# A Nystrom attention with a folded feed-forward network on one core: every stage cut into one step per engine, and a new written order

## The chip, the cores and the metric

The kernel runs on one core of a Trainium2 chip. A core has five engines that work side by side, each with its own queue of instructions that it takes strictly in order: TensorE (PE in the profile; its weight loads are shown as PEld), VectorE (DVE), ScalarE (ACT), GpSimd (POOL) and SyncE (SP), which here only issues transfers. Engines wait for each other through semaphores. The metric is the device time of one execution in microseconds; lower is better. The time given is the median of several executions.

## The reference

Eight batches of eight heads, 576 positions of 64 numbers each, go through a Nystrom approximation of attention with 32 landmarks; its output goes through a feed-forward network whose two halves are multiplied.

```python
q_lm = q.reshape(B, H, m, S // m, D).mean(axis=3)      # m = 32
k_lm = k.reshape(B, H, m, S // m, D).mean(axis=3)
A = sm(q, k_lm)          # sm: softmax of scaled products
Bm = sm(q_lm, k_lm)
C = sm(q_lm, k)
Z = Bm^T / (norm1(Bm) * norminf(Bm) + 1e-6)
for _ in range(6):
    Z = 2 * Z - Z @ Bm @ Z
attn = A @ Z @ C @ v
x = attn, heads side by side                            # 4608 x 512
h = (x @ w1) * (x @ w2) @ w3                            # 512 -> 1024
out = h @ w_out                                         # 1024 -> 512
```

## The kernel before

*Folding.* As nothing stands between w3 and w_out, the kernel first multiplies them into one matrix w34 (`fold`). w_out is split into a high and a low float16 half (`split`: ACT makes the high half at L510, DVE the low half at L511). Each 128 rows of w3 are turned by PE in two halves of four transposes (`turn` inside `fold`, L517) and split likewise (ACT L522, DVE L523). `product` multiplies them, three matmuls for each of 8 x 8 blocks (high by high, high by low, low by high, L530), into one PSUM bank per eight blocks, which ACT copies out (L533). Twelve matmuls on a tile of zeros (L599) stand at the start.

*Attention, per batch.* q and k come in through POOL's queue (L107), v through SP's (L126, L131). DVE turns q and k (`turn`, L143). `landmarks` sums groups of positions (DVE for batch 0, POOL for the others, L206 to L216). `exchange` swaps halves between partitions (by PE and ACT for batches 0 and 1, by small transfers on SP for the others). `scores_b` makes the 32 x 32 scores, `scores_c` and `scores_a` the long ones (32 matmuls of 32 x 32 each, L274 and L322), with exponentials on ACT (L255, L282, L328) and a DVE transpose (L284). `norms` (PE L290, DVE L293 to L297) and `squares` (PE L305) start the inverse; `inverse` has six steps (PE L399, then DVE L405 and, after DVE, ACT L410, which give the next step its operands). The inverse runs for one batch or two at once: CHAINS are (0), (1, 2), (3, 4), (5, 6), (7). `values` multiplies by v in three parts of 24 float32 matmuls (L344) and takes the sums in eight more (L349); the profile shows each float32 matmul as two, each with a weight load of its own, so that one batch's values are 320 rows on PE. `denominators`, `inverted`, `mixed` and `normalise` (PE L362, DVE L369, ACT L374, DVE L376, PE L382, DVE L385) give the scaled left factor `ahat`. `landmark_values` (PE L421, ACT L426, DVE L427) gives the middle factor `zt`.

*Network, per batch.* `project` multiplies `zt` by w1 or w2 (PE L442; ACT L446 or DVE L448 copy out): G0 and G2 are of w1, G1 and G3 of w2. `up` multiplies that by `ahat` (PE L455, four matmuls for each of 16 words): the w1 side is copied by ACT (L459), the w2 side multiplied into it by DVE (L461). `down` multiplies 128 positions by w34 (PE L495, eight matmuls), ACT copies out (L499), SP stores (L502). The last of the 36 `down` blocks is done in two halves.

*PSUM.* There are three tiles "big" of two banks, one "small" and one "acc", handed out in turn in the order of the text. A stage that takes a tile waits until the stage that had it has been read.

*The order.* Nothing schedules at run time or at build time: `manual_schedule` keeps the order in which the Python code emits. The string ORDER at the head has 575 words; the loop at L656 calls one function for each, for example `U3a.2` (`up`, eighth 3, w1 side, batch 2), `I4.1` (fifth step of the inverse of the chain of batch 1), `W0.17` (half a `down` block) or `F` (the next block of the fold). A function emits all of its work at once, its PE matmuls and behind them the ACT, DVE or POOL operations on their result. So one word fixes the place of that work on every engine's queue, relative to all other words. What stands before the loop (loads of w3, w_out, q, k of batches 0 and 1, w1 and w2, and DVE's constants at L162) is emitted first, in the order of the code; POOL's loads of q and k wait there behind a copy (`gate`, L603) that needs a tile of w_out.

Of the kernel before, what the change touches and what calls it, by code (L numbers as in the profile page):

```python
# [32 lines left out]
F F F F F F F F F F F F F TK0.0 F F F F F TQ0.0 TQ1.0 F F L3.3 F TK1.0 F F F F F SK0.0 SK1.0 F F  # L33
SQ0.0 P.4 F F F F L3.5 F L3.7 F F TQ0.1 TK0.1 SQ1.0 F F L3.6 TK1.1 F E.0 F B.0 F C0.0 SK0.1 N.0
F F F A0.0 R.0 FV.0 TQ1.1 F SK1.1 F I0.0 F F D.0 I1.0 F I2.0 Y0.0 Y1.0 SQ0.1 Y2.0 LK0.2 F X.0 F
I3.0 LK1.2 F F F I4.0 V0.0 V1.0 SQ1.1 LQ0.2 LQ1.2 E.1 F LK0.3 TK0.2 TK1.2 F LK1.3 I5.0 F V2.0
LV0.2 F TQ0.2 TQ1.2 A0.1 Z.0 SK0.2 LV0.1 LV1.1 F M0.0 LV2.1 F LV3.1 D.1 Y0.1 Y1.1 Y2.1 G0.0 G1.0
G2.0 M1.0 SK1.2 F SQ0.2 TK0.3 G3.0 TK1.3 C0.1 X.1 F F F F U0a.0 U0b.0 U1a.0 U1b.0 U2a.0 U2b.0
LQ0.3 TQ0.3 LQ1.3 LK0.4 U3a.0 LV1.2 V0.1 U3b.0 SQ1.2 E.2 U4a.0 U4b.0 B.1 U5a.0 U5b.0 N.1 V1.1
SK0.3 V2.1 R.1 U6a.0 U6b.0 TQ1.3 U7a.0 I0.1 M0.1 LK1.4 LQ0.4 U7b.0 W0.0 SK1.3 I1.1 W1.0 I2.1  # L40
A0.2 LV2.2 TK0.4 LV3.2 W0.1 I3.1 TK1.4 W1.1 I4.1 M1.1 LQ1.4 W0.2 TQ0.4 I5.1 W1.2 SQ0.3 SQ1.3
TQ1.4 Z.1 SK0.4 E.3 SK1.4 SQ0.4 LV0.3 C0.2 G0.1 D.2 G1.1 G2.1 W0.3 Y0.2 G3.1 V0.2 V1.2 Y1.2 V2.2
LV0.4 Y2.2 U0a.1 U0b.1 LV1.3 LK0.5 U1a.1 U1b.1 LV1.4 LK1.5 X.2 U2a.1 U2b.1 U3a.1 U3b.1 Z.2 SQ1.4
E.4 U4a.1 U4b.1 U5a.1 G0.2 TK0.5 U5b.1 U6a.1 U6b.1 M0.2 LQ0.5 LQ1.5 W1.3 U7a.1 LV2.3 U7b.1 LV3.3
M1.2 W0.4 G1.2 G2.2 G3.2 B.3 TK1.5 W1.4 U0a.2 A0.3 W0.5 U0b.2 U1a.2 LV2.4 D.3 Y0.3 Y1.3 SK0.5
U1b.2 Y2.3 C0.3 W1.5 LK0.6 U2a.2 U2b.2 U3a.2 W0.6 X.3 U3b.2 U4a.2 N.3 SK1.5 V0.3 V1.3 V2.3 R.3
U4b.2 TK0.6 W1.6 LV3.4 U5a.2 U5b.2 W0.7 TQ0.5 U6a.2 I0.3 M0.3 LK1.6 TQ1.5 W1.7 I1.3 SQ0.5 LQ0.6
U6b.2 W0.8 I2.3 W1.8 I3.3 U7a.2 U7b.2 W0.9 I4.3 M1.3 W1.9 I5.3 A0.4 LQ1.6 Z.3 C0.4 W0.10 G0.3
G1.3 G2.3 D.4 W1.10 Y0.4 LV0.5 SQ1.5 G3.3 E.5 LV1.5 U0a.3 U0b.3 Y1.4 W0.11 TK1.6 Y2.4 U1a.3
# [18 lines left out]
def kernel(  # L68
# [93 lines left out]
    def constants():  # L162
# [6 lines left out]
        for h in range(4):  # L169
            sl = slice(32 * h, 32 * h + 32)  # L170
            nc.vector.memset(mask4[sl, h, :], 1.0)
            for qd in range(2):
                nc.vector.tensor_copy(out=eye[sl, qd, :], in_=ident[sl, sl])
                nc.vector.memset(onesq[sl, qd, :, qd, h:h + 1], 1.0 / X64)
# [531 lines left out]
```

## Time and profile before

| | us |
|---|---|
| median of three executions | 264.64 (264.03 to 265.34) |
| profiled execution, first to last instruction (span) | 261.8 |
| median less span | 2.9 |
| PE busy | 251.5 |
| DVE busy | 173.8 |
| ACT busy | 134.7 |
| POOL busy | 103.2 |

The costliest groups on PE are `up` (L455, 512 matmuls, 73.1 us busy), `down` (L495, 264 matmuls into acc, 67.2) and the fold's products (L530, 168 into acc, 41.3). Busy times of groups overlap, since matmuls are pipelined.

By stretches of the span:

| stretch, us | PE busy | DVE busy | ACT busy | share of the 16 DMA engines |
|---|---|---|---|---|
| 0 to 10 | 8.29 | 8.70 | 5.07 | 0.81 |
| 10 to 50 | 39.48 | 26.16 | 16.84 | 1.06 |
| 50 to 100 | 46.48 | 36.24 | 23.81 | 0.73 |
| 100 to 180 | 79.74 | 60.74 | 48.30 | 0.72 |
| 180 to 262 | 77.51 | 41.98 | 40.72 | 0.38 |

A row of the profile gives line, engine, operation, output and inputs, shapes and count; behind the bar the busy time, the mean time of one in ns, and the idle time of the engine just before such instructions, with what ended it. A row of the timeline gives the start, the time taken, and in brackets the idle time before. "issue" means that the profile shows nothing that the engine waited for.

### The profile page before, as it was taken

The page shows a single profiled execution, that of the slowest core. Times are in us where ns is not written, and L with a number is a line of the kernel's source. Part 1 is how long each engine was busy: PE and PEld are TensorE (multiplying, and loading weights), DVE is VectorE, ACT ScalarE, POOL GpSimd, SP SyncE. Part 2 cuts the span into 40 slices and gives each one's busy share as a digit, 9 for nine tenths or more (in the row PEclk, how much of TensorE's full clock was granted, in tenths as well). Part 3 has the DMA queues.
Part 4 walks back from the last instruction along what each step waited for, and adds up shares of the span by engine and source line. Part 5 has one row for each costly group of instructions (what it writes and reads, how often), then busy time and mean ns, then how long its engine had stood idle before and what let it go on. Part 6 is the DMA issues. An engine that isn't in the chain of part 4 may idle for free.

```text
span 261.8 us, 10518 instructions
## 1 busy us (share of the span) xinstructions
PE 251.5 (96%) x4578; PEld 148.7 (57%) x4578; DVE 173.8 (66%) x352; ACT 134.7 (51%) x305; POOL 103.2 (39%) x134
## 2 busy tenths in 40 slices
PE   7999999998989999999999999999999999999993
PEld 3455554454556558557654674766476556656642
DVE  8765887556958687788856958767775656464410
ACT  4543236343652565576449546746646555455531
POOL 3630018998981999027092597504400000000000
PEclk9999999999999999999999999999999999999999
DMA  6999998999963448976668496933640713222355
GB/s 236 333 243 284 245 248 191 183 137 240 175 105 50 120 101 167 216 195 114 131 100 162 101 214 150 161 58 86 147 86 3 173 43 80 45 62 61 81 118 127
DMA packets 25070, 37.78 MB, mean 144 GB/s; under 512 B 4672, under 2 KB 13120, under 8 KB 25024
## 3 DMA queue, kind: packets, MB, share of 16 engines
q1 hardware_dynamic: 14704, 24.65, 36.9%
q0 software_dynamic: 9728, 11.54, 28.1%
q10 hardware_dynamic: 592, 0.92, 1.1%
q8 instruction: 36, 0.59, 1.0%
q14 instruction: 10, 0.08, 0.1%
HBM read 38.80 MB, written 9.44 MB: 184 GB/s over the span
## 4 chain that ended last, share of the span: by engine, by line
PE 89%; DVE 4%; ACT 3%; issue 1%; DMA 1%; SPq 0%; DVEq 0%; ACTq 0%
PE big L455 23%; PE acc L495 22%; PE acc L530 14%; PE big L442 5%; PE big L344 5%; PE big L399 4%; PE big L517 2%; PE small L530 2%; PE big L382 2%; PE small L421 2%; PE big L274 1%; PE big L495 1%; PE big L322 1%; DVE ab L461 1%; PE small L248 1%
## 5 line engine op out<-in xcount | busy, mean ns | idle before, releaser
L455 PE MATMUL big<-ahat,gt 128*128 128x288 f16 x512 | 73.1, 287 | 0.7 <-DVE ab L461 0.6
L495 PE MATMUL acc<-w,ab 128*128 128x512 f16 x264 | 67.2, 380 | 0.0
L461 DVE TENSOR_TENSOR ab<-a_sb,big 128x576 f16<-128x576 f16 x64 | 48.0, 750 | 27.2 <-ACT a_sb L459 16.8
L455 PEld LDWEIGHTS <-gt 128*128 128x128 f16 x512 | 48.3, 98 | 21.1 <-issue 3.1
L459 ACT CAST a_sb<-big 128x576 f16<-128x576 f32 x64 | 40.8, 640 | 33.9 <-PE big L455 32.9
L206 POOL TENSOR_TENSOR tr<-qkT 128x1024 f32<-128x1024 f16 x14 | 29.7, 2123 | 70.0 <-DVE qkT L143 69.8
L530 PE MATMUL acc<-wsp,w3t 128*128 128x512 f16 x168 | 41.3, 380 | 0.7 <-ACT w L533 0.5
L495 PEld LDWEIGHTS <-ab 128*128 128x128 f16 x280 | 25.3, 98 | 24.9 <-issue 3.5
L499 ACT ACTIVATE o_sb<-acc 128x512 f32<-128x512 f32 x33 | 19.8, 599 | 19.5 <-PE acc L495 19.1
L530 PEld LDWEIGHTS <-w3t 128*128 128x128 f16 x192 | 18.1, 98 | 18.9 <-issue 1.3
L143 DVE STREAM_TRANSPOSE qkT<-qkn 128x576 uint32<-128x576 uint32 x32 | 24.0, 763 | 2.0 <-DMA qkn<-in_k_dram 2.0
L448 DVE TENSOR_SCALAR gt<-big 128x1024 f16<-128x1024 f32 x16 | 19.1, 1211 | 3.1 <-PE big L442 3.0
L446 ACT ACTIVATE gt<-big 128x1024 f16<-128x1024 f32 x16 | 15.9, 1032 | 5.9 <-PE big L442 5.9
L211 POOL TENSOR_TENSOR tr<-tr 128x512 f32<-128x512 f32 x14 | 17.9, 1282 | 0.6
L442 PE MATMUL big<-wup,zt 64*32 64x512 f16 x512 | 17.4, 380 | 0.2 <-ACT en L282 0.2
L523 DVE SCALAR_TENSOR_TENSOR w3t<-big,w3t 128x512 f16<-128x512 f32 x16 | 11.0, 687 | 10.0 <-ACT w3t L522 10.0
L522 ACT ACTIVATE w3t<-big 128x512 f16<-128x512 f32 x16 | 9.5, 596 | 13.9 <-PE big L517 13.8
L284 DVE STREAM_TRANSPOSE ent<-en 128x576 f32<-128x576 f32 x16 | 12.1, 768 | 4.4 <-ACT en L282 4.4
L344 PE MATMUL big<-vt,ent 64*32 64x64 f32 x1152 | 14.2, 226 | 0.0
L282 ACT ACTIVATE en<-big 128x288 f32<-128x288 f32 x32 | 12.7, 411 | 2.9 <-PE big L274 2.7
L344 PEld LDWEIGHTS big<-vt,ent 64*32 64x32 f32 x1152 | 12.7, 105 | 2.0 <-ACT a_sb L459 0.5
L328 ACT ACTIVATE eat<-big 128x576 f16<-128x576 f32 x16 | 9.6, 652 | 7.3 <-PE big L322 7.3
(214 smaller groups left out, 285.2 us busy)
## 6 DMA issues: line engine op xcount, KB each, us to landing
out_dram<-o_sb SPq DMA_DIRECT2D x70, 128.0 KB, 2.5
vt<-in_v_dram SPq DMA_DIRECT2D x16, 288.0 KB, 5.3
vt<-in_v_dram SPq DMA_DIRECT2D x32, 144.0 KB, 4.0
qkn<-in_k_dram POOLq DMA_DIRECT2D x12, 288.0 KB, 5.4
qkn<-in_q_dram POOLq DMA_DIRECT2D x12, 288.0 KB, 4.9
w3f<-in_moe_w_dram SPq DMA_DIRECT2D x6, 512.0 KB, 6.7
wup<-in_moe_w_dram POOLq DMA_DIRECT2D x4, 512.0 KB, 25.3
wof<-in_moe_w_out_dram SPq DMA_DIRECT2D x6, 256.0 KB, 4.5
```

Of the source, the lines that this page charges most:

```text
L143: nc.vector.transpose(out=st["qkT"][:, t, prs].rearrange("p c r q e -> p (c r q e)").bitcast(U32), in_=st["qkn"][:, t, prs, :].rearrange(" ...
L206: add(out=tr, in0=x[:, :, 0:4, :], in1=x[:, :, 4:8, :], op=ALU.add)
L211: add(out=tr[:, :, 0:2, :], in0=tr[:, :, 0:2, :], in1=tr[:, :, 2:4, :], op=ALU.add)
L344: nc.tensor.matmul(psV[32 * o:32 * o + 32, qd, 0:64], ent[sl, pr, r, :], vt[sl, pr, 64 * r:64 * r + 64], start=(r == 0), stop=(r == RT - 1 ...
L442: nc.tensor.matmul(psG[o:o + 32, qd, :], zt[rs, i, h, :], wup[rs, h, w, fs], start=(i == 0), stop=(i == 1), tile_position=(64 * qd, o))
L448: nc.vector.tensor_scalar(out=g[:, :, w, fs], in0=psG, scalar1=1.0 / ZS, scalar2=None, op0=ALU.mult)
L455: nc.tensor.matmul(p[:, c, 0:HS], st["g"][:, qd, w, 128 * j:128 * j + 128], st["ahat", qd][:, c, :], start=(qd == 0), stop=(qd == 1))
L459: nc.scalar.copy(out=st["a_sb"], in_=p[:, :, 0:HS])
L461: nc.vector.tensor_tensor(out=st["ab"][:, j, st["t0"]:st["t0"] + S].rearrange("p (c s) -> p c s", c=2), in0=st["a_sb"], in1=p[:, :, 0:HS], ...
L495: nc.tensor.matmul(pso[:, :], ab[:, j, t0:t0 + 128], w34[:, j, :], start=(j == 0), stop=(j == 7))
L499: nc.scalar.activation(out=o_sb, in_=pso, func=AXF.Copy, scale=1.0 / (X64 * X64))
L530: nc.tensor.matmul(psW[j][:, :], turned[j, c // 4][:, a, c % 4, :], wsp[:, b, c, :], start=(c == 0 and a + b == 0), stop=(c == 7 and a == 1))
```

## The change

1. The functions become generators: a `yield` stands between the part of a stage that one engine does and the next part. A word of ORDER now names a whole stage (`up` of both sides and their product is `U3.2`, a whole `down` block is `W.17`, `values` is `V.2`) and stands in the order once for each part; each time the loop meets it, the next part is emitted. The place of PE's part, of ACT's and of DVE's can thus be chosen one by one. Two parts of one engine remain apart where they were (`values` in three, `down` in two halves of four matmuls).
2. ORDER is written anew with 1,096 such steps. It now also holds what was emitted before the loop: the parts of the fold (S splits, T turns, F products), DVE's constants (KC, in eleven parts), the loads of w1 and w2 (LW), of q and k for batches 0 and 1 in halves (LK, LQ), the loads of w3 and w_out (L, LO, P), the gate (GT, now one in front of several loads of q and k) and the warm matmuls behind the first seven (K).
3. What each operation computes, its shapes, the tiles and the number of buffers stay as they were.

The core of the diff:

```diff
-    def up(st, j, w):
-        p = big()
-        for qd in range(2):
-            for c in range(2):
-                nc.tensor.matmul(p[:, c, 0:HS], st["g"][:, qd, w, 128 * j:128 * j + 128],
-                                 st["ahat", qd][:, c, :], start=(qd == 0), stop=(qd == 1))
-        if w == 0:
-            st["a_sb"] = po.tile([128, 2, HS], FP16, name="a_sb", bufs=2)
-            nc.scalar.copy(out=st["a_sb"], in_=p[:, :, 0:HS])
-        else:
-            nc.vector.tensor_tensor(
-                out=st["ab"][:, j, st["t0"]:st["t0"] + S].rearrange("p (c s) -> p c s", c=2),
-                in0=st["a_sb"], in1=p[:, :, 0:HS], op=ALU.mult)
+    def up(st, j):
+        for w in range(2):
+            p = big()
+            for qd in range(2):
+                for c in range(2):
+                    nc.tensor.matmul(p[:, c, 0:HS], st["g"][:, qd, w, 128 * j:128 * j + 128],
+                                     st["ahat", qd][:, c, :], start=(qd == 0), stop=(qd == 1))
+            yield
+            if w == 0:
+                a_sb = po.tile([128, 2, HS], FP16, name="a_sb", bufs=2)
+                nc.scalar.copy(out=a_sb, in_=p[:, :, 0:HS])
+                yield
+        nc.vector.tensor_tensor(
+            out=st["ab"][:, j, st["t0"]:st["t0"] + S].rearrange("p (c s) -> p c s", c=2),
+            in0=a_sb, in1=p[:, :, 0:HS], op=ALU.mult)
...
     def inverse(ch, it):
...
+        yield
         if not last:
...
+            yield
             ch["sz"] = pz.tile([128, 4, 64], FP32, name="sz_", bufs=2)
             nc.scalar.copy(out=ch["sz"][:, x].rearrange("p (a b) m -> p a (b m)", a=2), in_=psv)
...
+    def turned_w3(j, cc):
+        wt = big()[:, 0, :]
+        for c in range(4):
+            f = 512 * cc + 128 * c
+            nc.tensor.transpose(out=wt[:, 128 * c:128 * c + 128], in_=w3f[j][:, f:f + 128], identity=ident[:, :])
+        yield
...
+        nc.scalar.activation(out=hi, in_=wt, func=AXF.Copy, scale=WS)
+        yield
+        nc.vector.scalar_tensor_tensor(out=lo, in0=wt, scalar=WS, in1=hi,
+                                       op0=ALU.mult, op1=ALU.subtract)
...
+    def gated(j):
+        nc.gpsimd.tensor_copy(out=gate, in_=(wof[4] if j == 0 else w3f[j])[:, 0:1])
...
     for word in ORDER.split():
-        name, _, b = word.partition(".")
-        if name == "F":
-            next(fd, None)
...
+        if word not in live:
...
+            work = started(word)
...
+            live[word] = work
+        if live[word] is not None:
+            next(live[word], None)
```

In the new file a product of the fold is L539, its turn L526 (ACT L530, DVE L532), a split L517 and L519, a step of the inverse L396 (DVE L403, ACT L409), the scores L261 and L316, the projection L445 (ACT L450, DVE L452), `up` L460 (ACT L465, DVE L467), `down` L502 (ACT L508, SP L512).

The head of the two orders, to the first products:

```diff
-F F F F F F F F F F F F F TK0.0 F F F F F TQ0.0 TQ1.0 F F L3.3 F TK1.0 F F F F F SK0.0 SK1.0 F F
...
+T0.0 T0.0 T0.1 S.0 KC T0.1 S.1 K S.2 LK1.0 T0.1 K GT.0 K S.0 T0.0 S.4 S.1 K F.0 T1.0 F.1 F.0 T1.0
+S.3 LO.6 S.2 S.5 S.4 F.0 F.1 T1.0 L.2 S.3 T1.1 F.0 LO.7 S.6 T1.1 KC T1.1 F.1 T0.2 S.7 T1.2 LK0.0 S.7
...
```

(`T0.1` is the first half of the second 128 rows of w3: the number at the name is the half, the one behind the point the rows. Its three places are PE's, ACT's and DVE's part.) Before, the first `F` emitted split 0, turn (0, 0), three warm matmuls, split 1, turn (1, 0), two warm matmuls and the first block of products, each with all of its engines' parts.

## The prediction

> **What bounds the kernel now.** I read the page first, then the table of waits on PE alone, then stretches of the timeline.
>
> ```profile
> span 261.8 us, 10518 instructions
> PE 251.5 (96%) x4578; PEld 148.7 (57%) x4578; DVE 173.8 (66%) x352; ACT 134.7 (51%) x305; POOL 103.2 (39%) x134
> PEclk9999999999999999999999999999999999999999
> PE 89%; DVE 4%; ACT 3%; issue 1%; DMA 1%; SPq 0%; DVEq 0%; ACTq 0%
> ```
>
> PE is busy for 96% of the span, at full granted clock, and carries 89% of the chain that ended last. No other engine comes near. What PE waits for is therefore all there is to win without taking matmuls away:
>
> ```profile
> PE big L349 <- issue: 1.3, 1, 1.3
> PE big L599 <- DVE warm L594: 1.2, 1, 1.2
> PE small L290 <- DVE bm L260: 1.0, 1, 1.0
> PE big L455 <- DVE ab L461: 0.6, 2, 0.4
> PE acc L530 <- ACT w L533: 0.5, 2, 0.2
> ...
> PE big L382 <- ACT gt L446: 0.3, 1, 0.3
> ```
>
> The table goes on with 0.3, 0.2, 0.2 and 0.2. The 1.2 of L599 is the start and stays, as do 0.3 and 0.2 of the first 8 us. So 2.8 us of waits on DVE and ACT and 1.3 us of "issue" can go, 4.1 us in all.
>
> The start, where weights are folded:
>
> ```profile
> 5.53 0.60 ACT L522 ACTIVATE w3t<-big 128x512 f16<-128x512 f32 x1 [0.19 <-PE big L517]
> 6.44 0.63 DVE L511 SCALAR_TENSOR_TENSOR wsp<-wof,wsp 128x512 f16<-128x512 f32 x1
> 6.64 0.60 ACT L522 ACTIVATE w3t<-big 128x512 f16<-128x512 f32 x1
> 6.87 0.63 PE L530 MATMUL acc<-wsp,w3t 128*128 128x512 f16 x2
> 6.98 0.68 DVE L523 SCALAR_TENSOR_TENSOR w3t<-big,w3t 128x512 f16<-128x512 f32 x1
> 7.72 1.19 PE L530 MATMUL acc<-wsp,w3t 128*128 128x512 f16 x4 [0.22 <-DVE w3t L523]
> ```
>
> A product needs the high halves from ACT (about 0.6 us each) and the low halves from DVE (0.63 and 0.68 us). The third product waits for DVE's second low half; from 7.72 on PE runs without a pause.
>
> The inverse, a chain PE, DVE, ACT, PE:
>
> ```profile
> 88.16 0.45 PE L399 MATMUL big<-sz__1520,tz__1518 32*32 32x64 f32 x32
> ...
> 88.74 0.29 DVE L405 TENSOR_TENSOR tz__1588<-big,eye 128x128 f32<-128x128 f32 x1 [0.83 <-PE big L399]
> ...
> 89.12 0.37 ACT L410 COPY sz__1590<-big 128x256 f32<-128x256 f32 x1 [0.34 <-DVE tz__1588 L405]
> ...
> 89.54 0.30 PEld L399 LDWEIGHTS big<-sz__1590,tz__1588 32*32 32x32 f32 x32 [0.46 <-ACT sz__1590 L410]
> ```
>
> ACT's copy ends at 89.49 and the next step starts at 89.54. Its last matmul started 0.24 us after 88.16, so a step follows 1.14 us after that last start. The other full-speed pairs of two-batch chains in the trace lie at 1.11 to 1.15. The order of before put 0.9 to 1.3 us of other PE work there, so this costs it nothing.
>
> **The change, part by part.** Both programs hold the same matmuls (the page's 4578, which count float32 ones twice) and the same ACT and DVE operations; only places differ. POOL gets five more gate copies (the row of "gate" is 0.51, the smallest POOL copies 0.2) and four more DMA issues of 0.75 us; POOL has 158 us of idle and nothing of PE waits on it at those places, so 0 (without that cover at most 5 x 0.51 + 4 x 0.75 = 5.6, in the first 50 us).
>
> *Start.* Before, five warm matmuls separate the first turns of w3; now two turns follow each other, then four warm matmuls. ACT makes the high halves in the order turned tile (0,0), wout 0, turned tile (1,0), wout 1. DVE's first low half is now that of turned tile (1,0), ahead of wout 0 and of turned tile (0,0), which the first product needs. With the rows above: tile (1,0) is on PE at 5.97 (its load sets that), PE done at 6.6, ACT 6.75 to 7.35, then DVE 7.4 to 8.1, 8.1 to 8.75 and 8.75 to 9.43. So the third product comes at 9.5 instead of 7.72. PE then has the same four groups of transposes behind it at 13.35 in both, but 15 products against 23.3; 8.3 x 0.216 us (the trace's start to start) = 1.8, and one warm matmul of 0.2 comes later: **+2.0**. Bounds: 1.0 if DVE and ACT are each a third quicker than this string, 2.8 if the k load that now goes out ahead of POOL's gate (288 KB; at the 333 GB/s of the second slice 0.9 us) lies wholly before w3.
>
> *Inverse.* By the queue order, six steps now follow the previous with little between: once one block of 32 small score matmuls in batch 0's chain, once the same in the chain of batches 1 and 2, three times four matmuls of L455 (4 x 0.122 us plus 0.25 for two changes of array shape), once 16 of L442 and eight of L362. Start to start that is 0.55, 0.55, three times 0.75, and 1.0, against 1.14 (one-batch chains: 0.90 at their quickest). Waits: 0.35 + 0.59 + 3 x 0.39 + 0.1 = **+2.2**. Bounds 1.2 (only the two blocks of score matmuls and 0.1 each for the others) and 3.5 (DVE has a stream transpose of 0.77 queued between two of its steps in two of them).
>
> *Waits that go.* Of the 2.8 us, those of L455 and L382 have more PE work ahead of them now, one of two drains of acc and the norm step still look tight: **-2.0**, bounds -2.8 and +0.5 (that as many new ones come as go, and a little more, as DVE's 3.3 us of constants move from the first 6.5 us into 20 to 40 us of PE work, where DVE rows then sum to 22.3 us instead of 16.8).
>
> *Dense runs.* The 1.3 us of issue fell at 58.61 to 59.89, in the third part of batch 0's values (L344, L349). One of the 36 instruction packets of 16 KB came within a microsecond before; in the 8 us ahead none had come, while software-queue packets filled the DMA engines. 9,201 PE rows in 36 packets is 256 a packet. In the new order that part is split, but four of eight batches keep all 320 rows of values in one run, and the shortest packet's worth of PE work falls from 2.8 us to 2.0 (about 110 us, batch 3). I take -1.3 and half a microsecond back: **-0.8**, bounds -1.3 and +1.3 (that another packet is as late).
> [...]
>
> *Changes of array shape.* PE's order changes shape 139 times instead of 150. At 61.83 three L530 are followed by L382 of the same shape after 0.64 us; at 62.72 by L362 of another after 0.74: 0.1 for going in. Coming out costs between 0 and 0.2. Eleven fewer: between -0.5 and -1.7, **-1.0**, nearer the sum of both as most small runs that merged lost a way in and a way out.
>
> *Tail.* PE's last matmul ends 4.2 us before the span does, in both orders behind the same last half tile: 0.
>
> Sum: 2.0 + 2.2 - 2.0 - 0.8 - 1.0 = +0.4, a span of 262.2 against 261.8. The median of the runs shown, 264.64, is 2.9 above that span; so 265.1.
>
> **The rivals.**
> *Faster: the tight places are covered.* For: of the places in before that look tight by the same count (64 negative ones against 83 now), most cost nothing. Against: the start's string has no spare work in it. -2.8 - 1.3 - 1.0 with 1.0 at the start and 0.5 elsewhere: -3.6, 261.0.
> *Slower: DVE becomes the bound of the first 60 us.* Place: the stretch of 20 to 40 us of PE work with 22.3 us of DVE work. For: DVE is in order, and the exps' transposes, norms and inverse steps of batch 0 queue behind the constants. It decides if the surplus of 2.3 us hasn't been worked off when the values of batch 0 start: the forecast plus 2.3 is 267.4. Against: 5 to 20 us has 12.4 us of DVE work in 15, 45 to 55 has 5.6 in 10.
> *Slower: w1 comes late.* Both halves of w1 are issued after batch 1's first POOL sums, some 46 us by text, against 13 before. Before, wup took 25.3 us to land behind k and q; with that, projection at some 60 us (56 of PE work ahead of it and four of waits) would wait 11 us (276). With the 3 us apart at which the four landed before, it is there by 55. Little chance.
> *Slower: the clock.* The row: warm matmuls start 0.426 us apart until 4.2 us and 0.216 after 5.3. Between 7.6 and 9.4 PE now does a single product. If it falls back to 0.426 for another 3 us, some seven matmuls cost 0.21 more: +1.5, 266.6. [...]
> *The change isn't what it says:* if dense runs stop PE as before, the term of -0.8 is 0, which gives 265.9 and lies within the forecast's own range.
>
> **How the numbers follow.** Forecast 0.32; covered places 0.29; DVE 0.25; w1 0.07; clock 0.07. A measurement here tells 0.5% from nothing, 1.3 us, so the forecast itself is no change and takes in a little of either side. Faster 0.30, within 0.30, slower 0.40. All lows of the bounds together are 1.0 + 1.2 - 2.8 - 1.3 - 1.7 = -3.6, all highs +7.6; the range holds the low case and the DVE case and leaves out w1: 261.0 to 269.2. The forecast's own range is 263.3 to 266.3.
>
> **What will show it.** Start: the third L539 product near 9.5, and L532 on DVE in the order (1,0), wout, (0,0). Inverse: PE or weight loads of L396 waiting for ACT's L409 at about six places, 0.3 to 0.6 each. Issue: no wait in batch 0's values, perhaps one near 110 us. Waits of PE on DVE with a mean over 0.5 us between 25 and 65 us would make the DVE rival right. If the first products start before 8 us, or PE's idle time falls under 4 us in all, the forecast is wrong.

## The result and the profile after

The changed kernel takes 274.33 us (median of four, 273.6 to 276.67) against 264.53 for the kernel before (264.03 to 265.34): a ratio of 1.0387, interval 1.0338 to 1.0436. A median takes in every execution; a ratio leaves out those more than 1.5% above the quickest of the same kernel, so the two can differ below. Forecast were 265.1 us and a range of 261.0 to 269.2. The profiled execution has a span of 271.6 us, 9.8 more than before.

The head of the page of the changed kernel: span, busy times of the engines, granted clock by slices of 6.8 us, and shares of the chain that ended last.

```profile
span 271.6 us, 10492 instructions
PE 253.5 (93%) x4578; PEld 150.3 (55%) x4578; DVE 175.4 (65%) x352; ACT 133.0 (49%) x305; POOL 106.5 (39%) x143
PEclk9999999999998899999999999999999999999999
PE 69%; POOL 9%; DVE 9%; DMA 6%; issue 3%; ACT 1%; SPq 1%; ACTq 0%; DVEq 0%; POOLq 0%
```

PE has the same matmuls and is busy 2.0 us longer, so nearly 8 of the 9.8 us are waits. POOL, which was not on the chain before, holds 9% of it, DVE 9% instead of 4%, and the clock has a dent near 90 us. The first eight lines of what PE waits for (us in total, times, longest):

```profile
PE big L337 <- issue: 2.2, 2, 1.5
PE big L396 <- DVE tz__1441 L305: 2.1, 1, 2.1
PE small L282 <- DVE bm L247: 2.0, 1, 2.0
PE big L460 <- issue: 1.6, 1, 1.6
PE big L526 <- DMA w3f<-in_moe_w_dram: 1.2, 3, 0.6
PE big L592 <- DVE warm L588: 1.2, 1, 1.2
PE acc L539 <- DVE wsp L519: 0.9, 1, 0.9
PE big L396 <- ACT sz__1541 L409: 0.5, 1, 0.5
```

Two waits on DVE of 2.0 and 2.1 us and three on "issue" (0.6, 1.5 and 1.6 us) make 7.9 us. The waits of before on the norms of batches 1 and 2, on the drains and on `ab` are gone.

**What DVE did.** The timeline of the changed kernel ahead of the first of the two (start, time taken, engine, line, operation):

```profile
36.75 0.76 DVE L166 STREAM_TRANSPOSE qkT<-qkn 128x576 uint32<-128x576 uint32 x1
37.54 2.29 DVE L625 CAST selc<-selr 32x128 f16<-32x128 f32 x2
37.59 2.15 POOL L190 TENSOR_TENSOR tr<-qkT 128x1024 f32<-128x1024 f16 x1 [1.93 <-DVE qkT L166]
39.84 0.19 DVE L630 TENSOR_TENSOR eye<-eye 128x32 f32<-128x32 f32 x1
...
42.47 0.23 DVE L247 TENSOR_TENSOR bm<-small,rbs 128x64 f32<-128x64 f32 x1
42.85 0.41 PE L282 MATMUL small<-bm,mask 128*128 128x64 f32 x2 [2.04 <-DVE bm L247]
```

and around the second:

```profile
82.93 0.42 DVE L302 TENSOR_TENSOR sz__1439<-small,nrn 128x256 f32<-128x256 f32 x1
83.38 2.34 DVE L305 TENSOR_TENSOR tz__1441<-sz__1439,eye 128x128 f32<-128x128 f32 x1
83.43 2.13 POOL L190 TENSOR_TENSOR tr<-qkT 128x1024 f32<-128x1024 f16 x1
...
85.87 0.46 PE L396 MATMUL big<-sz__1439,tz__1441 32*32 32x64 f32 x32 [2.12 <-DVE tz__1441 L305]
```

A pair of casts takes 0.35 us elsewhere in this trace and the addition of L305 0.29 in its free instance of this shape. Both end within 0.2 us of the end of POOL's first sum of landmarks. DVE looks busy; as I read it, it is held. The addition's row begins 0.05 us ahead of POOL's, so the start that is shown does not tell which of the two is held. The kernel before made these casts in its first 6.5 us, where POOL makes no sums:

```profile
3.98 1.45 DVE L186 CAST selc<-selr 32x128 f16<-32x128 f32 x8
```

Of DVE's other operations none is stretched over POOL's sums: 13 transposes of L166 (0.762 us on average over sums, 0.766 apart from them), 18 of `up` (L467, one input in PSUM: 0.749 and 0.750), 17 reciprocals of L365 from PSUM (0.458 and 0.452). Held are the cast out of SBUF (2.15 us beside a sum of 2.15) and the addition with both inputs in SBUF (2.34 beside a sum of 2.13). My theory, below called the lock, is an estimate from these rows: such a DVE instruction and a POOL sum do not run at the same time, and DVE's lasts until the sum is done. What in the hardware keeps them apart is not shown.

**The clock.** The windows of the changed kernel behind the second wait (PE, PEld, DVE, ACT, POOL busy, then granted clock, DMA share, GB/s):

```profile
84.00:85.00 1.00, 0.00 (x0) 0.00 (x0) 1.00 (x1) 0.00 (x0) 1.00 (x1) 1.00 1.11 188
...
87.00:88.00 1.00, 1.00 (x5) 0.53 (x4) 0.39 (x1) 0.14 (x1) 0.92 (x2) 0.50 0.96 214
88.00:89.00 1.00, 1.00 (x6) 0.64 (x5) 0.00 (x0) 0.36 (x1) 0.92 (x2) 0.50 1.12 228
89.00:90.00 1.00, 1.00 (x35) 0.47 (x33) 0.33 (x1) 0.28 (x1) 0.80 (x3) 0.50 1.16 205
```

After 2.1 us without PE work the clock is half from 86.8 to 90.2 us: another 1.7 us lost. After the wait before 42.85, of 2.04 us, it stays full. The two differ in where they lie. In each of the 16 profiles (before, after and the 14 experiments) all changes of the granted clock are whole multiples of 3.413 us apart; in after they are at 4.88, 86.80, 90.22 and 271.12. On that grid the second wait lies wholly within one stretch (83.39 to 86.80), while a border at 42.43 cuts the first and leaves at most 1.62 us of it on one side. Over the 16 profiles, all seven stretches at full clock with 2.1 us or more without PE work are followed by half clock, none with less than 1.3 is, and between 1.3 and 1.9 both occur. So how much of one stretch is idle counts, more than the length of the wait; an exact limit is not shown.

**The issue waits.** I counted all rows of PE in the trace (matmuls, weight loads and some 45 rows of its sequencer, in order of start) and set the starts of the 16 KB instruction packets beside them. In the 16 profiles there are 45 issue waits of over 0.15 us. All 45 end at a row that is 193 or 194 beyond a multiple of 256. So I read the waits as PE running dry at the end of a block of 256 rows whose successor has not come. There are as many packets as blocks (36 and 36 in after), so I set one to each; most start after PE has begun the block; in stretches with few rows some start shortly before it (2 of 36 in before, 4 in after). Some blocks:

| kernel | block begins | its packet starts | later by | next block begins | of it waiting |
|---|---|---|---|---|---|
| before | 54.17 | 57.59 | 3.42 | 59.89 | 1.27 |
| after | 74.40 | 77.02 | 2.62 | 79.88 | 0.61 |
| after | 123.25 | 126.93 | 3.68 | 129.19 | 1.54 |
| after | 129.19 | 131.67 | 2.48 | 133.85 | 1.59 |
| after, no wait | 102.71 | 103.80 | 1.09 | 106.51 | 0 |

The two waits behind q and k loads, in the timeline of after:

```profile
129.19 0.85 PE L337 MATMUL big<-vt,ent 64*32 64x64 f32 x66 [1.54 <-issue]
133.85 0.66 PE L460 MATMUL big<-ahat,gt 128*128 128x288 f16 x4 [1.59 <-issue]
```

In the 45 cases the wait ends 2.2 to 3.0 us after the packet starts. So a wait has two ingredients: a packet that starts late (2.5 us and more after the block, in the rows above with loads on the DMA engines, whose share is 1.12 from 54.2 to 57.6 us in before, 1.07 from 74 to 77 and 1.22 from 123 to 127 in after, and 0.73 from 129 to 132; 1.09 us in the row without a wait, where the share is 0.05) and a block that PE gets through quickly. The second alone makes none: the block of after at 176.8 takes 2.3 us, its packet starts 0.4 us ahead of it, and PE does not wait.

**Where the 9.8 us arise.** Every matmul was counted with the mean start-to-start time of its stage in before; the table shows how much later than in before PE had done the same amount of work.

| PE work done, us | 15 | 30 | 40 | 55 | 70 | 90 | 100 | 150 | 210 |
|---|---|---|---|---|---|---|---|---|---|
| reached in before at | 21.5 | 37.2 | 49.7 | 70.4 | 90.9 | 117.0 | 128.0 | 191.3 | 257.0 |
| after, later by | 2.0 | 1.9 | 3.9 | 1.6 | 5.3 | 5.4 | 8.9 | 9.4 | 9.8 |
| all_four, later by | 1.2 | 1.9 | 2.4 | 1.5 | 1.2 | 2.0 | 2.4 | 2.9 | 3.3 |

Start +2.0; first hold +2.0; then 2.3 won back (before's issue wait at 60 among it); second hold with half clock +3.7; between 90 and 100 of work +3.5, of which the two issue waits are 3.1; a slow 0.9 to the end.

### The profile page after: what moved, and what is told of

It reads as the page before. It is cut to its first block, busy times and chain, and to the rows that moved or that the text cites. A ratio compares the mean times of both kernels' runs of the same rounds, so it can differ in the third digit from the quotient of the medians.

```text
span 271.6 us, 10492 instructions
## 1 busy us (share of the span) xinstructions
PE 253.5 (93%) x4578; PEld 150.3 (55%) x4578; DVE 175.4 (65%) x352; ACT 133.0 (49%) x305; POOL 106.5 (39%) x143
## 4 chain that ended last, share of the span: by engine, by line
PE 69%; POOL 9%; DVE 9%; DMA 6%; issue 3%; ACT 1%; SPq 1%; ACTq 0%; DVEq 0%; POOLq 0%
PE big L460 22%; PE acc L502 21%; PE big L445 5%; PE big L337 4%; DMA w3f<-in_moe_w_dram 4%; PE big L396 3%; PE acc L539 3%; POOL tr L190 2%; POOL tr L195 2%; DMA lm<-lm 2%; DVE qkT L166 1%; PE big L378 1%; PE small L422 1%; PE big L502 1%; PE small L539 1%
## 5 line engine op out<-in xcount | busy, mean ns | idle before, releaser
L460 PE MATMUL big<-ahat,gt 128*128 128x288 f16 x512 | 74.8, 289 | 1.7 <-issue 1.6
L467 DVE TENSOR_TENSOR ab<-a_sb,big 128x576 f16<-128x576 f16 x64 | 47.0, 750 | 32.1 <-PE big L460 27.9
L502 PE MATMUL acc<-w,ab 128*128 128x512 f16 x264 | 67.5, 381 | 0.2 <-ACT o_sb L508 0.2
L460 PEld LDWEIGHTS <-gt 128*128 128x128 f16 x512 | 48.4, 99 | 22.7 <-issue 3.7
L465 ACT CAST a_sb<-big 128x576 f16<-128x576 f32 x64 | 39.9, 640 | 39.9 <-PE big L460 27.6
L539 PE MATMUL acc<-wsp,w3t 128*128 128x512 f16 x168 | 40.9, 379 | 1.2 <-DVE wsp L519 0.9
L502 PEld LDWEIGHTS <-ab 128*128 128x128 f16 x280 | 25.7, 98 | 25.3 <-issue 3.5
L539 PEld LDWEIGHTS <-w3t 128*128 128x128 f16 x192 | 18.2, 98 | 20.1 <-DVE w3t L532 1.8
L508 ACT ACTIVATE o_sb<-acc 128x512 f32<-128x512 f32 x33 | 19.8, 601 | 12.4 <-PE acc L502 11.4
L166 DVE STREAM_TRANSPOSE qkT<-qkn 128x576 uint32<-128x576 uint32 x32 | 24.2, 764 | 0.6 <-DMA qkn<-in_k_dram 0.5
L452 DVE TENSOR_SCALAR gt<-big 128x1024 f16<-128x1024 f32 x16 | 19.3, 1216 | 3.8 <-PE big L445 3.8
L450 ACT ACTIVATE gt<-big 128x1024 f16<-128x1024 f32 x16 | 16.1, 1024 | 6.5 <-PE big L445 6.5
L337 PE MATMUL big<-vt,ent 64*32 64x64 f32 x1152 | 15.3, 225 | 2.2 <-issue 2.2
L445 PE MATMUL big<-wup,zt 64*32 64x512 f16 x512 | 17.3, 379 | 0.0
L532 DVE SCALAR_TENSOR_TENSOR w3t<-big,w3t 128x512 f16<-128x512 f32 x16 | 10.8, 678 | 9.3 <-ACT w3t L530 9.3
L129 POOL DMA_DIRECT2D qkn<-in_q_dram x16 | 11.5, 721 | 11.5 <-DVE qkT L166 8.4
L382 DVE TENSOR_TENSOR ahat<-eat,big 128x576 f16<-128x576 f16 x16 | 11.9, 749 | 3.8 <-PE big L378 3.8
L530 ACT ACTIVATE w3t<-big 128x512 f16<-128x512 f32 x16 | 9.5, 595 | 7.1 <-PE big L526 6.8
## 6 DMA issues: line engine op xcount, KB each, us to landing
out_dram<-o_sb SPq DMA_DIRECT2D x70, 128.0 KB, 2.4
```

The source lines that it names most:

```text
L166: nc.vector.transpose(out=st["qkT"][:, t, prs].rearrange("p c r q e -> p (c r q e)").bitcast(U32), in_=st["qkn"][:, t, prs, :].rearrange(" ...
L337: nc.tensor.matmul(psV[32 * o:32 * o + 32, qd, 0:64], ent[sl, pr, r, :], vt[sl, pr, 64 * r:64 * r + 64], start=(r == 0), stop=(r == RT - 1 ...
L445: nc.tensor.matmul(psG[o:o + 32, qd, :], zt[rs, i, h, :], wup[rs, h, w, fs], start=(i == 0), stop=(i == 1), tile_position=(64 * qd, o))
L452: nc.vector.tensor_scalar(out=g[:, :, w, fs], in0=psG, scalar1=1.0 / ZS, scalar2=None, op0=ALU.mult)
L460: nc.tensor.matmul(p[:, c, 0:HS], st["g"][:, qd, w, 128 * j:128 * j + 128], st["ahat", qd][:, c, :], start=(qd == 0), stop=(qd == 1))
L465: nc.scalar.copy(out=a_sb, in_=p[:, :, 0:HS])
```

## The experiments

Times are medians, ratios are to the kernel before.

### tz_psum: the addition of L305 without a second SBUF input

```diff
-        nc.vector.tensor_tensor(out=tz_[:, x], in0=sz_[:, x, 0:32],
-                                in1=eye2.unsqueeze(1).to_broadcast([128, 2 * n, 32]), op=ALU.add)
+        for i in range(2 * n):
+            nc.vector.scalar_tensor_tensor(out=tz_[:, i], in0=psR[:, 64 * i:64 * i + 32],
+                                           scalar=ch["nrn"][:, i:i + 1], in1=eye2,
+                                           op0=ALU.mult, op1=ALU.add)
```

> The changed kernel with one operation written otherwise: 2I plus the scaled square, which begins each inverse (L305), is made from the product in PSUM and the norms, by one scalar_tensor_tensor for each 32 columns (two or four of them) instead of one tensor_tensor that reads two SBUF tiles. Theory, that POOL's sum of landmarks holds a DVE instruction with two SBUF inputs: the 2.34 us at 83.4 us become four instructions of 0.1 to 0.2 us, PE's wait of 2.1 us at 85.9 falls below 0.5, and the clock, which was granted at half for 3.2 us after that wait, stays full; span 267.7 to 268.9 instead of 271.6, time about 270.8. Rival, that DVE is late because its queue holds too much work: DVE has some 0.4 us more to do before the first inverse step, so the wait stays at 2 us or grows, and the span stays at 271.6 to 272.0.

272.92 us, 1.0344 (1.0320 to 1.0368). The timeline of this kernel at the same place:

```profile
82.93 0.42 DVE L300 TENSOR_TENSOR sz__1440<-small,nrn 128x256 f32<-128x256 f32 x1
83.27 0.72 DVE L304 SCALAR_TENSOR_TENSOR tz__1442<-small,nrn,eye 128x32 f32<-128x32 f32 x4
```

0.72 us instead of 2.34, PE's wait there is 0, the clock between 80 and 100 us is 1.00 (0.93 between 75 and 100 after). The lock theory holds, the rival falls. But the time falls by 1.4 us, not 3.5: this profile has a new issue wait of 1.27 us at 91 and new waits on the landmark exchange (lm) of 0.46 and 0.97 us, at 75.5 and 112.8.

### casts_ahead: two parts of the constants ahead of the turn

```diff
-... KC LQ1.2 F.4 TK0.1 LK0.2 T1.4 TK1.1 KC F.4 LK1.2 KC T0.5 ...
+... KC LQ1.2 F.4 KC KC TK0.1 LK0.2 T1.4 TK1.1 F.4 LK1.2 T0.5 ...
```

> The changed kernel with two parts of the constants (the last cast of selc and the part with eye2 and bt) four to seven words earlier, so that DVE makes them ahead of the turn whose end releases POOL's first sum of landmarks, not right behind that turn. DVE has the same work in the same stretch, from 35 to 43 us. Theory of the lock: the cast takes 0.2 us instead of 2.15, DVE's work up to the scaled scores ends 2 us sooner, PE's wait of 2.04 us at 42.85 falls below 0.4; span 269.4 to 270.0. Rival, too much DVE work: the same sum of work ends at the same time, the wait stays above 1.5 us and the span at 271.2 or more.

273.01 us, 1.0349 (1.0310 to 1.0389). All four remaining casts last 0.73 us together and the wait at 42.85 is gone, with the same DVE work in the same stretch: the lock again. The span came out at 272.3, not 270. DVE now stands for 1.6 us before a turn whose k load isn't there, so that the addition of L305 comes 46.25 us into the run, into the next POOL sum (45.55 to 47.68): held to 1.5 us, PE waits 1.46 for it:

```profile
34.58 0.73 DVE L623 CAST selc<-selr 32x128 f16<-32x128 f32 x4
46.25 1.52 DVE L303 TENSOR_TENSOR tz__637<-sz__635,eye 128x64 f32<-128x64 f32 x1
```

Issue waits sum to 5.9 us, and behind one of 2.1 us the clock is half from 133.9 to 137.4.

### start_lows: DVE's low halves in the order of before

```diff
-... LK1.0 T0.1 K GT.0 K S.0 T0.0 S.4 ...
+... LK1.0 K GT.0 K S.0 T0.0 T0.1 S.4 ...
```

> The changed kernel with DVE's low half of the turned tile (1,0) behind those of wout 0 and of the turned tile (0,0), as the kernel before has it; one word moved by five places. The prediction's term for the start, 2.0 us: the third product of L539 starts at 8.0 to 8.3 instead of 9.33, and 1.0 to 1.3 us stay gained at 25 us and in the span (270.3 to 270.6). Rival, that the landing of w3 sets the pace from 10 to 15 us: the third product is as early, but PE waits that much longer for a w3 tile at 14.7, and the span stays within 0.3 of 271.6.

274.55 us, 1.0392 (1.0353 to 1.0431): no gain. In its profile the third product starts at 9.55, because PE works at half rate there until 10.6 us (warm matmuls and products start 0.43 us apart; in the profile of after half rate ends at 4.9 us, and they start 0.22 apart). In all_four, which has the same order, PE is at full rate and the third product starts at 7.78 us; of the 1.1 us that it is ahead of after by 5 us of work, 0.8 are left at 15 and 22 us, as PE then waits 0.33 and 0.54 us for w3. So DVE's order costs about what was expected, and it matters only if the clock is up. The profile also has half clock from 44.8 to 48.2, behind the same hold of the casts.

### loads_later: four q and k loads out of the way of two instruction packets

```diff
-... LQ0.7 ... LK0.7 ... LK1.6 U4.2 SQ0.5 SQ1.5 LK0.6 U6.2 M0.3 ...
+... LK0.6 ... SQ0.5 SQ1.5 U6.2 M0.3 GQ LQ0.7 LK1.6 LK0.7 ...
+    def gate_q():
+        nc.gpsimd.tensor_copy(out=gate, in_=sts[3]["ahat", 0][:, 0, 0:1])
```

> The changed kernel with four q and k loads of batches 6 and 7 at other places in POOL's queue: the half of batch 6 that is needed first takes the place of the first, at 120 us; the other three go out behind a small POOL copy that reads a result of 133 us, so that they move between 134 and 144 us instead of 120 and 129. Theory, that PE's two issue waits of 1.5 and 1.6 us come from instruction packets that stand behind these loads: the packets at 126.9 and 131.7 us start within 1.5 us of PE's reaching the block of 256 rows before (3.7 and 2.5 now), and the waits at 129.2 and 133.9 sum to at most 0.7 us instead of 3.1; span 268.4 to 269.3. Rival, that a dense run of small matmuls outruns the fetch whatever else is moved: the waits stay above 2.4 us together and the span at 271 or more.

272.06 us, 1.0324 (1.0265 to 1.0383). The packets of those two blocks start 1.34 and 0.99 us after the block (3.68 and 2.48 before), the waits are 0 and 0.35 us instead of 1.54 and 1.59. So these waits come from packets behind loads. The same profile has an issue wait of 1.3 us at 95, half clock from 94.8 to 98.2, both holds, and at 19.8 us a wait of 1.9 us for a low half of w_out.

### no_locks: tz_psum and casts_ahead together

> The edits of tz_psum and casts_ahead together, so that no DVE instruction with two SBUF inputs and no cast out of SBUF stands next to POOL's sums. Both theories: no DVE instruction is stretched by more than 0.3 us, PE's waits on DVE at 42.9, 47.9 and 85.9 us fall below 0.5 each and the clock stays full. Theory that the holds add up: 2.0 + 2.1 us of waits and 1.6 us of half clock go, time 268.6 us. Rival, that PE only arrives sooner at instruction packets and landmark transfers that are not there yet, as in tz_psum, where new issue and lm waits of 1.3 and 1.0 us ate half the gain: waits on issue and lm sum to over 5 us in the profile, time 270.5 to 272.

273.91 us, 1.0333 (1.0270 to 1.0396), with single times from 271.3 to 278.0. No DVE instruction is held. The time is hardly under that of after, so the holds do not add up to 5.7 us of time. The profile is of the longest of the four (278.0), which the ratio leaves out; the other three take 271.3 to 274.4. It has issue waits of 8.2 us in five places, and its packets are up to 5.4 us late. What the three quicker executions met in place of the holds is not shown.

### all_four: the four edits together

> The four edits so far together (tz_psum, casts_ahead, start_lows, loads_later). If their gains add up: 274.3 less 5.7 of holds and half clock, 3 of issue and 1 at the start, 264.6 us. If waits are only handed on to later packets and transfers: 268 to 270.5, with issue and lm waits of over 3 us in sum between 50 and 140 us. No DVE hold in either case.

268.85 us, 1.0217 (1.0141 to 1.0294); some 5 us of the 9.8 are back (5.5 by the medians, 4.5 by the ratios). The profiled execution, the quickest, lost 3.3 us to before (last line of the table above). Issue waits there are 1.17, 0.38, 0.32 and 0.30 us.

### before_cast and before_casts: a hold made in the kernel before

```diff
             in_=st["qkn"][:, t, prs, :].rearrange("p c f -> p (c f)").bitcast(U32))
+        st["turned"] = st.get("turned", 0) + 1
+        if st["b"] == 1 and st["turned"] == 3:
+            spare = consts.tile([128, 128], FP16, name="spare")
+            for c in range(4):
+                sl = slice(32 * c, 32 * c + 32)
+                nc.vector.tensor_copy(out=spare[sl, :].rearrange("p (h m) -> p h m", m=32),
+                                      in_=eye[sl, 0, 0:4].unsqueeze(2).to_broadcast([32, 4, 32]))
```

before_cast has the first of the four copies alone.

> The kernel before with one added DVE instruction, a cast of 32 partitions by 128 out of SBUF like those of selc, right behind the turn whose end releases POOL's first sum (37.6 us); nothing uses its result. Theory of the lock: the cast lasts 2.0 to 2.2 us, as long as POOL's sum, instead of the 0.21 us of such a cast elsewhere, and DVE's reciprocal at 39.6 comes 0.8 to 1.0 us later; time 0 to 1 us up. Rival, that the casts of the changed kernel were long for another reason (a wait for data, instructions that came late): the cast lasts 0.2 to 0.3 us and nothing else moves.

264.31 us, 1.0011 (0.9987 to 1.0036). The cast took 0.17 us, from 39.86; POOL's sum began at 40.03. It was there first and decided nothing.

> The kernel before with four such added casts behind the same turn (32 partitions by 128 each, into a tile that nothing uses) instead of one. The single cast of before_cast began while the turn was still ending and was done (0.17 us) when POOL's sum began, so it decided nothing. Theory of the lock: the first cast is as short as that one; the second or third, not begun when the sum starts, lasts about 2.1 us, until the sum ends; DVE's reciprocal of L265 comes 1.0 to 1.6 us later, time 0 to 1 us up. Rival: four casts of about 0.2 us each, 0.7 us in all, and DVE free before POOL's sum ends.

270.46 us (one execution; before 264.66). The timeline of before_casts, DVE's rows and POOL's:

```profile
39.49 4.53 DVE L151 CAST spare<-eye 32x128 f16<-32x128 f32 x4
39.65 2.13 POOL L213 TENSOR_TENSOR tr<-qkT 128x1024 f32<-128x1024 f16 x1 [19.61 <-DVE qkT L143]
41.73 0.18 POOL L631 CAST vt<-qkn 128x4 f32<-128x4 f16 x1
41.88 1.25 POOL L218 TENSOR_TENSOR tr<-tr 128x512 f32<-128x512 f32 x1
44.05 0.17 DVE L265 RECIPROCAL rbs<-rbs 128x2 f32<-128x2 f32 x1
```

Four casts of 0.17 us take 4.53: POOL's instructions run in between, one after the other, while casts wait. The span of this one execution is 6.9 us longer than that of before; 1.2 of it arise at 21 us, ahead of the casts, so four tiny instructions that nothing needs cost some 5.7 us. PE waits 2.85 us for what stands behind them on DVE, and then works at half clock from 44.1 to 50.9 us, two stretches of the grid; the windows:

```profile
42.00:44.00 2.00, 0.00 (x0) 0.00 (x0) 1.99 (x2) 1.57 (x8) 1.85 (x2) 1.00 0.34 55
44.00:46.00 2.00, 1.31 (x5) 0.79 (x6) 1.83 (x6) 0.00 (x0) 1.42 (x3) 0.53 1.05 281
46.00:48.00 2.00, 2.00 (x6) 0.76 (x5) 1.23 (x5) 0.00 (x0) 0.00 (x0) 0.50 1.06 239
48.00:50.00 2.00, 2.00 (x51) 0.95 (x49) 0.00 (x0) 0.06 (x1) 0.00 (x0) 0.50 0.85 184
```

I had expected at most 1 us in time: the hold is as the theory has it (twice as long, even), the price of PE's pause wasn't.

### before_rows and after_rows: 124 more rows on PE

```diff
-    warm_up(7)
+    warm_up(5)
+    for i in range(64):
+        g = h = i % 4
+        nc.tensor.matmul(psw[32 * h:32 * h + 32, 0, 0:32], warm[32 * g:32 * g + 32, 0:32],
+                         warm[32 * g:32 * g + 32, 0:32], start=True, stop=True,
+                         tile_position=(32 * g, 32 * h))
```

> The kernel before with two of its seven first warm matmuls replaced by 64 of 32x32 (about 1 us either way): 124 rows of PE's program more ahead of everything else, nothing else touched. Theory, that PE runs dry at fixed counts of rows (193 beyond a multiple of 256 in all eight waits on issue of before and after) when the 256 rows up to there take less than some 3.6 us: moved by 124 rows, eight of before's blocks hold a whole run of values or scores and take 1.3 to 3.1 us (none under 3.8 now), so there are seven to nine waits on issue of 1 to 2.5 us near 76, 93, 119, 146, 164, 189 and 215 us, again at 193 rows beyond a multiple of 256, 11 to 17 us in sum; time 274 to 281 us against 264. Rival, that a dense run makes PE wait by itself, wherever it stands in the program: the waits stay as they are (one of 1.3 us at 60), time 263.5 to 265.5.

280.71 us, 1.0626 (1.0560 to 1.0691): 16.6 us more with 64 matmuls that take 0.69 us at the start. The waits of before_rows on PE, and two rows of its timeline:

```profile
PE big L344 <- issue: 3.7, 2, 1.9
PE small L305 <- issue: 3.2, 2, 1.7
PE big L322 <- issue: 2.7, 1, 2.7
PE big L399 <- issue: 1.6, 1, 1.6
```

```profile
233.54 1.60 PE L344 MATMUL big<-vt,ent 64*32 64x64 f32 x140
...
236.93 0.34 PE L399 MATMUL big<-sz__4558,tz__4556 32*32 32x64 f32 x16 [1.61 <-issue]
```

Six waits of 1.5 to 2.7 us, 11.1 in sum, all at row 193 or 194, at 85, 130, 161, 182, 209 and 237 us, inside the dense runs where the count had put seven to nine. The wait of before at 60 us is gone, as its values no longer end a block. At 234 us the DMA engines are nearly idle (0.06 of their time between 234 and 235, 0.25 from 225 to 240) and the packet starts 0.8 us after the block, and still 256 rows in 1.5 us of PE work run PE dry. Not all of the 16.6 us are these waits, though (before has 1.3 us of them). Half clock lasts until 10.7 us here and 5.1 in before, which makes PE some 2.3 us later by 10.8 us; whether the two warm-up products fewer or chance does it is not separated (k3_later, with the start of before, is at half clock until 6.5; loads_later, with that of after, until 9.5, after until 4.9). And the clock is half again from 79.0 to 82.4 and from 160.9 to 164.3. So a dense run is no wait by itself; a block boundary behind it is.

after_rows is the same edit in the changed kernel.

> The changed kernel with the edit of before_rows: two warm matmuls of the start replaced by 64 of 32x32, 124 rows of PE's program more. What is told apart is how much of 'dense runs spread out' is worth where the boundaries of 256 rows do not fall by chance into sparse work. Spread runs are worth something there: the same 124 rows cost the kernel before 16.6 us and cost this one 5 to 9 (its blocks of under 3.6 us sum to 8 us more than now), time 279 to 283. Rival, the runs are as dense as before to the fetch: 14 us or more, time 288 or more. In both cases the issue waits stand at 193 or 194 rows beyond a multiple of 256.

285.84 us, 1.0659 (1.0585 to 1.0734), single times 280.3 to 288.9; two of the four (288.6 and 288.9) are left out of the ratio. The other two, 280.3 and 283.1, are 7.4 us above after on average, 7.2 by the ratios. Against 16.6 in before_rows, that is the time that the first theory named. But it does not follow that spreading the small matmuls eases the fetch: the issue waits of this profile still sum to 9.4 us, in six waits of 0.9 to 2.5, against 11.1 in before_rows. The runs of the new order are still dense to the fetch, and after had 3.7 us of such waits to begin with where before had 1.3.

### all_four_rows: boundaries where the count likes them best

```diff
-    for _ in range(7):
+    for _ in range(3):
         warm_up()
+    for i in range(118):
+        g = 32 * (i % 4)
+        nc.tensor.matmul(psw[g:g + 32, 0, 0:32], warm[g:g + 32, 0:32], warm[g:g + 32, 0:32],
+                         start=True, stop=True, tile_position=(g, g))
```

> All four edits with 228 rows of PE's program more at the start (four warm matmuls replaced by 118 of 32x32), the shift for which the rows of all_four's profile give the fewest blocks of 256 rows under 4.6 us (before 140 us) and 3.6 us (behind): 4.9 us of shortage in sum instead of 7.5. If the position of the boundaries is what is left: time 1.5 to 3 us under the 268.85 of all_four. If it is the lateness of packets behind loads, or the colder start takes it back: 268 to 270.

269.15 us, 1.0174 (1.0139 to 1.0209). Not one issue wait is left in the profile, and the time is the same. Three things stand against the gain: the start is colder (full clock from 10.2 us instead of 3.9 in all_four; PE is 0.9 us later by 15 us of work), PE now waits for the landmark exchange, and the clock is half from 75.1 to 78.5. The first lines of its waits:

```profile
PE small L231 <- DMA lm<-lm: 2.4, 3, 0.9
PE big L526 <- DMA w3f<-in_moe_w_dram: 1.3, 2, 1.1
```

### weights_early: w1 and w2 at 22 to 25 us

```diff
-... LQ0.1 T0.4 ... LW.1 ... LW.1 ... LW.0 ... LW.0 ...
+... LQ0.1 LW.0 LW.0 LW.1 LW.1 T0.4 ...
```

> All four edits with the four loads of w1 and w2 (2 MB) issued at 22 to 25 us, near where the kernel before has them, instead of 34 to 48 us. Theory, that data moved between 45 and 62 us makes the instruction packets there late: the packets of the blocks that begin near 42, 50 and 55 us start within 1.5 us instead of 2.3, 2.3 and 1.6; the issue wait of 1.2 us at 54.6 goes, time 266.5 to 268. Rival: the DMA engines are full from 10 to 40 us, so w3 and the first q and k come later by what w1 and w2 take (2 MB at some 250 GB/s is 8 us), PE waits for w3 or the turns 2 us or more in 20 to 45 us, time above 270.

275.52 us, 1.0419 (1.0387 to 1.0451). The issue wait near 55 us is gone as expected, but PE waits 7.4 us at 54 us for an operand of the first inverse step (L304 on DVE). The rival was right in its main point: in after the DMA engines are full there already (share 1.06 to 1.18 between 20 and 40 us), and what comes in ahead came at the cost of what is needed next. DVE stood for 8.9 us, until 52.46, for a k load: the k loads issued there land 19.8 us after their issue (12.6 in all_four). The clock is half from 51.3 to 61.5. The wait for w3 that the rival also named stayed small, 0.6 us.

### k3_later and pool_relief: the two last waits moved

k3_later is the kernel before with LK0.3 and LK1.3 behind SK0.2 in ORDER instead of ahead of TK0.2 and I5.0.

> The kernel before with the two k loads of batch 3 issued behind POOL's next sum (about 58 us) instead of ahead of it (53.8). Theory: the instruction packet that was 3.4 us late behind the q and k loads issued at 52.4 to 55.3 comes earlier, PE's issue wait of 1.3 us at 59.9 shrinks to 0 to 0.5, nothing else has to wait for these loads (they are turned at 67 us); time 0.5 to 1.2 us under the kernel before. Rival, the q loads alone keep the packet back, or the next packet (block from 59.9) is now the late one: no change within 0.4 us.

264.79 us, 1.0021 (0.9996 to 1.0045): no change. The packet is still 3.28 us late, the wait 1.2 us; so the q loads of 52.6 us seem enough to keep it back.

pool_relief is all_four_rows with LQ1.4 and LK0.3 behind SQ1.2.

> all_four_rows with the loads of LQ1.4 and LK0.3 issued behind POOL's landmark sums of q of batch 2 instead of ahead of them. Theory, that POOL's own queue, busy without a pause from 44 to 68 us with sums, loads and gates, is what PE's scores of batches 1 and 2 wait for next: the sums end 1.4 us sooner, so do the landmark exchange and PE's first two lm waits (1.5 us in sum at 74 to 75 us), which fall below 0.5; time 1 to 1.5 us under 269.15. Rival, that the exchange is slow because its packets stand behind the data loads: the lm waits stay at 1.2 us or more and the time within 0.5 of 269.15.

269.73 us, 1.0201 (1.0169 to 1.0233). The lm waits are gone, as the theory of POOL's queue has it, and the time isn't: an instruction packet that starts 5.0 us after its block makes PE wait 3.9 us at 81, with half clock from 82.6 to 86.0 behind it. No order tried beats the kernel before.

## Why the prediction was wrong

By its own steps, against the 9.8 us of span:

| step | forecast | found |
|---|---|---|
| start | +2.0 | +2.0 |
| inverse | +2.2 | +1.7 |
| waits that go | -2.0 | -2.4, and two new ones +4.2 |
| dense runs (issue) | -0.8 | +2.5 |
| changes of array shape | -1.0 | about +0.2 |
| tail | 0 | 0.0 |
| half clock behind a wait | a rival, at the start | +1.7, at 87 us |

*Start: right.* DVE's low halves began at 7.38, 7.99 and 8.59 (forecast 7.4, 8.1, 8.75), the third product at 9.33 (9.5). start_lows and all_four show that DVE's order carries it only while PE's clock is up.

*Inverse: right, a little large.* Six waits of L396 on ACT's copy, 0.5 to 0.2 us each.

*Waits that go: here the prediction failed first.* The old waits did go. But the step let DVE's moved work cost at most half a microsecond by adding up DVE's time (22.3 us instead of 16.8 between 20 and 40), and the rival "DVE becomes the bound" priced it at 2.3 by the same sum. Its sign was met: PE waits on DVE with a mean over 0.5 us between 25 and 65 us. Its cause was not. casts_ahead keeps the sum of DVE's work and loses the wait; tz_psum adds DVE work and loses the other. What was missing is whom DVE runs beside: moving the constants from the first 6.5 us, where POOL makes no sums, to the instant at which a turn releases POOL's sum turned a cast of 0.2 us into 2.15. The sum put POOL at 0 because it has 158 us of idle and nothing of PE waits on it at those places; that looked at POOL's queue alone, not at what POOL's sums do to DVE. Even the sum of all the upper bounds, +7.6, stays under the 9.8 of span: these two holds were in no term.

*Dense runs: here it failed again.* That the wait is a late instruction packet was read rightly. But the step took dense runs as the cause that splitting removes, and counted the shortest packet's worth of PE work (2.0 us at 110) as half a microsecond. What decides is where a multiple of 256 rows falls and how late the packet behind it is. The old order happened to lie well: by the borders that the waits show, none of its blocks takes under 3.8 us of PE work, and 124 rows more bring it waits of 11.1 us (and, with a colder start and half clock, 16.6 us of time). Any reordering draws anew, and this one drew blocks of 4.4 and 3.1 us at 123 and 129 us, just behind q and k loads. That the new order drew badly and the old one well is chance as far as the prediction goes.

*Changes of array shape: not found.* Start to start beyond a stage's own rate, summed where the stage changes, is 23.6 us over 282 changes in before and 23.8 over 307 in after (an estimate from the rows' starts). A change of shape costs 0.148 us on average in before (150 of them) and 0.153 in after (139), 0.95 us less in all. Of the changes of stage within one shape, 186 of 198 in before and 207 of 222 in after lie within 0.02 us of the stage's own rate; the others sum to 1.6 us in before and 2.4 in after, which counting changes of shape alone missed. (These are the same kind of estimate for every change of line, with waits of over 0.1 us taken off; by them the term is -0.2.)

*Clock.* It fell back as the rival said, but behind a hold that wasn't foreseen, and not by the length of the wait alone: 2.12 us within one stretch of the grid were enough in after, 2.04 us cut by a border were not. The same wait of 2.0 us on DVE is followed by half clock in start_lows and after_rows, where one stretch has 1.7 and 1.8 us without PE work, and not in tz_psum and loads_later, where it has 1.4 and 1.2.

That the whole comes out near 9.9 of 9.8 doesn't make the terms independent. tz_psum, casts_ahead and pool_relief show that a wait taken away is often paid again: as a late packet, as an exchange that is not there, as another hold. How much of the 9.8 us any one edit is worth therefore stays open; together, the four edits are worth some 5. All four give back 0.8 of the 2.0 us of the start; against the 1.7 us of the inverse no edit was made, so that size is the table's alone.

## What to carry to other kernels

Before moving a DVE instruction, look at which POOL instruction runs beside its new place: here a cast within SBUF lasted 2.15 us and an addition of two SBUF tiles 2.34, about as long as POOL's sums beside them (2.15 and 2.13) and not 0.2 and 0.29; with one input read from PSUM the addition's four parts took 0.72. Before believing that a new order of small matmuls is better or worse, count PE's rows in blocks of 256, at whose ends all 45 issue waits lie here, and compare the PE time of each block with how late its instruction packet is; add some rows at the start as a test. Where several things arrive just in time, price an edit by what PE meets next, not by the wait removed.

## What was not expected of the hardware

- Four casts of 0.17 us, next to POOL's work, last 4.53 us, and PE, 2.85 us without work, then runs at half clock for 6.8 us: some 5.7 us in all, in one execution, from 0.7 us of work.
- PE's rows come in blocks of 256, and the packet of the next block mostly starts only after a block has begun: all 45 issue waits in 16 profiles are at 193 or 194 beyond a multiple of 256. Blocks of 256 rows in 1.5 to 1.6 us of PE work end in waits of 1.6 to 1.7 us even with packets only 0.7 to 0.9 us after the block's begin (before_rows at 130 and 237, after_rows at 207 and 237); in before_rows the DMA engines are nearly idle there between 234 and 235 us (0.06).
- In all 16 profiles the granted clock changes only at multiples of 3.413 us from its other changes, so two pauses of PE of nearly one length, 2.12 and 2.04 us in after, can differ in what follows: half clock for 3.4 us, or none.
